# Weight sums of w1 and w2 made at their conversion, and another order of matmuls in the last group of u times w_out

## The chip, the cores and the metric

The kernel runs on one core of a Trainium2 chip. The core has a tensor engine for matmuls (PE, with PEld for its weight loads), a vector engine (DVE), a scalar engine (ACT), GpSimd (POOL) and SyncE (SP), from whose queue this kernel starts its DMAs. Each engine works through its own list of instructions in order and waits at semaphores for the others. Matmuls read their operands from the on-chip memory SBUF and write to PSUM. The metric is the device time of one execution in microseconds (us).

## The reference

```
p_packed = softmax_attention(p, k, v)          # 8 batches x 8 heads, 32 pack rows, width 64
attn     = softmax_attention(q, p_packed, p_packed)
x  = attn as [4608, 512]                        # 8 x 576 tokens
x  = (silu(x @ w_gate) * (x @ w_val)) @ w_out   # d_ff 1536
y  = ((x @ w1) * (x @ w2)) @ w3 @ w_out2        # d_ff 1024
```

q, k, v and p are float32. The weights of both expert layers arrive as 64-bit floats and are turned into float32 on the chip.

## The kernel before, in words

**Numbers.** Every large product is made with three matmuls: each factor is split into a high part (a cast on ACT, names ending in h) and a low part (the difference, on DVE or POOL, names ending in l), and high x high, high x low and low x high are added up in PSUM. The splits of most tiles are made by the helper `split` (L93) with `sub` (L89), so they carry those lines in the profile.

**First expert layer.** The 8 batches are worked off in 4 pairs P, and for each pair d_ff is cut into 12 tiles f of 128. A step is one (P, f). In it, `c_mm` (L409) makes c, a small product of the packed attention with w_gate and w_val, for the next tile; ACT casts it to ch (L420) and DVE subtracts to cl. For each of the two batches of the pair `stage1` makes the gate's product pg and the value's product pv (L441, 12 matmuls of 288 columns each), ACT takes Silu of pg (L446), DVE multiplies by pv (L450) and the result u is split into uh (ACT) and ul (POOL). Three tiles f make a group g of `stage3` (L660): u of these three times w_out, six PSUM tiles px (j = 0 to 5) of 18 matmuls of 384 columns. Each px is then added to acc (L682), and after the last group stored to a DRAM buffer X2d. `stage3` of a group runs in the step after the group's last tile, in two halves; so of three steps two are short (7.6 us) and one is long. The last group of the last pair has no step after it and runs in a loop of its own (L938).

All of pc, pg, pv, px and the small products pw of the next layer share one PSUM pool `ps` with four buffers of two banks.

**Conversions beside it.** Weights still to be converted go through a list `raw_q`: loaded by SP into a "raw" buffer (five of them), converted by `conv` with one operation on ACT (L346) and two on DVE (L347, L350). In the second and third pair one tile of w1 or w2 is converted per step (16 tiles of 128 x 512, `w12_conv`), from the second pair's tile 3 to the third pair's tile 6, and stored to a DRAM buffer w12d.

**Second expert layer.** Stage 5 works in 6 token groups g, and in each over 8 tiles f of 128 (for w1 and w2 together), by a scheme of seven products (`PROD`): instead of eight block products with w1 and w2, seven with the blocks A11, A12, A22 and the sums S1 to S4 of the blocks. A product is 6 matmuls of 384 columns (L981), so a tile f has 42. In group 0 the sums (`ws_sums`, L770 to L773, DVE) and the seven splits (`ws_block`: ACT casts, DVE and POOL subtract in turn) of tile f+1 are made while tile f runs, and are stored to wsd; from group 1 on they are loaded from there (`ws_load`). ACT takes results out of PSUM (s, L996), DVE and POOL combine them. The token side, x2r loaded from X2d, goes through `x2_prep` (sums on DVE, splits on ACT and DVE); that of group 0 is made in the last steps of the fourth pair. Stage 7 (L1035) multiplies by w3 @ w_out2 (L1045, 144 matmuls of 512 columns per group).

**The order.** Up to the end of the first layer a scheduler that is part of the framework sets each engine's order, from its own estimates and from a few pins in the program (`pin`). Stage 5 and 7 stand in `tc.manual_schedule`, where each engine's order is that of the code.

Of the kernel before, what the change touches and what calls it, by code (L numbers as in the profile page):

```python
# [38 lines left out]
def packed_attention_moe_kernel(  # L39
# [40 lines left out]
    GF = 3  # L80
# [20 lines left out]
    w12d = tc.dram_tile([NF2, 128, 2, ND, 128], F32, name="w12d")  # L101
# [180 lines left out]
    w12_list = [(x, c, h) for h in range(2) for x in range(2) for c in range(ND)]  # L282
# [12 lines left out]
    def raw_src(key):  # L295
        what, *at = key.split("_")
        at = [int(x) for x in at]
        if what == "wo2":
            c, kk = divmod(at[0], NH)
            return w_out2[512 * c:512 * c + 512, :].rearrange("(i k a) n -> k i a n", k=NH, a=32)[kk]  # L300
        if what == "w3":
            c, r = at
            return w3[128 * r:128 * r + 128, 512 * c:512 * c + 512].rearrange(
                "(b rr) (i n) -> i b rr n", rr=4, i=4)
        if what == "w":
            return (w_gate, w_val)[at[1]][:, 128 * at[0]:128 * at[0] + 128].rearrange(
                "(k p) n -> p k n", p=128)
        if what == "wo":
            return w_out[128 * at[0]:128 * at[0] + 128, :]
        x, c, h = w12_list[at[0]]  # L310
        return (w1, w2)[x][128 * c:128 * c + 128, 512 * h:512 * h + 512]
# [5 lines left out]
    def raw_load():  # L317
        if raw_at[0] < len(raw_q):
            key = raw_q[raw_at[0]]
            src = raw_src(key)  # L320
            raw_at[0] += 1
            blocks = src.shape[0] == 4
            t = vc.tile([128, 512] if blocks else [128] + list(src.shape[1:]), I64, tag="raw",
                        name=f"raw_{key}", bufs=5)
            if blocks:
# [5 lines left out]
            raw_t.append((key, t))  # L331

    def conv(key, t):
# [23 lines left out]
        if not in_front[0]:  # L357
            raw_load()
# [300 lines left out]

    def stage3(P, g, e):  # L660
        for j in range(ND // 2 * 3 // 2 * e, ND // 2 * 3 // 2 * (e + 1)):
            t = psum(f"px{P}_{g}_{j}")
            for n in range(GF):
                f = GF * g + n
                uh, ul = (x.rearrange("p b a s -> p (b a s)") for x in u_pair[P, f])
                wh, wl = wo_t[P, f]
                for w, x, first, last in (
                    (wh, uh, n == 0, False), (wh, ul, False, False), (wl, uh, False, n == GF - 1),
                ):
                    for h in range(2):  # L670
                        d, c = divmod(2 * j + h, 3)
                        nc.tensor.matmul(  # L672
                            t[:, h, 0:CW], lhsT=w[:, 128 * d:128 * d + 128], rhs=x[:, CW * c:CW * c + CW],
                            start=first, stop=last,
                        )
            if g == 0:
                o = up.tile([128, 2, CW], F32, tag=f"acc{j}", name=f"acc{P}_{j}", bufs=1)
                nc.scalar.copy(o, t[:, :, 0:CW])
                acc[j] = o
            else:  # L680
                o = acc[j]
                nc.vector.tensor_tensor(out=o, in0=o, in1=t[:, :, 0:CW], op=ALU.add)  # L682
            if g == NG - 1:
                for h in range(2):
                    d, c = divmod(2 * j + h, 3)
                    t0 = 2 * S * P + CW * c
                    if j % 3 == 1:
                        nc.sync.dma_start(X2d[d, :, t0:t0 + CW], o[:, h])
                    elif h == 0:
                        nc.sync.dma_start(X2d[d, :, t0:t0 + 2 * CW], o.rearrange("p h s -> p (h s)"))  # L690


    def w12_conv(i):
        x, c, h = w12_list[i]
# [62 lines left out]
    x2_t, x2r_t, w12r_t, wsrc, ws_t, wg_at = {}, {}, {}, {}, {}, []  # L757

    def load_w12(f):
        t = xp.tile([128, 2, 2, 256], F32, tag="wf", name=f"w12r{f}")  # L760
        nc.sync.dma_start(t.rearrange("p x k n -> p x (k n)"), w12d[f].rearrange("p x c n -> p x (c n)"))
        w12r_t[f] = t

    def ws_sums(f):
        t = w12r_t.pop(f)
        a11, a12, a21, a22 = (t[:, x, kh] for x in range(2) for kh in range(2))
        sa = vl.tile([128, 2, 256], F32, tag="vu", name=f"wsa{f}")
        sb = vl.tile([128, 2, 256], F32, tag="vu", name=f"wsb{f}")
        tt = nc.vector.tensor_tensor
        tt(out=sa[:, 0], in0=a21, in1=a22, op=ALU.add)  # L770
        tt(out=sa[:, 1], in0=sa[:, 0], in1=a11, op=ALU.subtract)
        tt(out=sb[:, 0], in0=a11, in1=a21, op=ALU.subtract)
        tt(out=sb[:, 1], in0=a12, in1=sa[:, 1], op=ALU.subtract)  # L773
        wsrc[f] = {"A11": a11, "A12": a12, "A22": a22, "S1": sa[:, 0], "S2": sa[:, 1],
                   "S3": sb[:, 0], "S4": sb[:, 1]}
# [11 lines left out]
    def ws_block(f, k):  # L787

        t = ws_tile(0, f, k)
        split(t[:, 0], t[:, 1], wsrc[f][PROD[k][1]], sub_on="pool" if k % 2 else "dve")  # L790
        if f:
            nc.sync.dma_start(wsd[f, k], t.bitcast(F32).rearrange("p h (d n) -> p h d n", d=2))

    def ws_load(g, f, k):
        t = ws_tile(g, f, k)
        nc.sync.dma_start(t.bitcast(F32).rearrange("p h (d n) -> p h d n", d=2), wsd[f, k])
# [60 lines left out]
    for n, (P, f) in enumerate(steps):  # L857
# [59 lines left out]
        if P == NPR - 1:  # L917
# [53 lines left out]
    def stage5(g, f):  # L971
# [79 lines left out]
    load_wo3(0)  # L1051
    with tc.manual_schedule(engines=M0):
        for g in range(NG2):
            for f in range(NF2):
                stage5(g, f)
                if g == 0:
                    if f + 2 < NF2:
                        ws_sums(f + 2)
                    if f + 3 < NF2:
                        load_w12(f + 3)  # L1060
# [47 lines left out]
```

## Time and profile before

| | before |
|---|---|
| time, median of 3 runs | 1379.38 us (1378.85 to 1380.13) |
| profiled execution: time | 1378.52 us |
| profiled execution: span | 1376.7 us |
| mean granted clock of PE | 0.995 |
| busy share: PE, DVE, ACT, POOL | 98%, 48%, 42%, 28% |
| DMA | 230.28 MB, mean 167 GB/s |

PE is busy nearly all the time; the others have half of their time free. The page's chain of work that ended last lies on PE for 85% of the span. Times in the rows below are from the span's start, in microseconds. Neighbouring instructions of one kind are drawn together in a timeline: its "x2" at the end counts them, and the second number is their time together. A bracket at the end of a row is the idle time before it and what ended it.

### The profile page before, as it was taken

To read this page: it belongs to the slowest core of one execution; us is meant where nothing else is said; L and a number is where in the kernel's file an instruction comes from. 1 tells how busy PE (TensorE), PEld (TensorE's weight loads), DVE (VectorE), ACT (ScalarE), POOL (GpSimd) and SP (SyncE) were. 2 spreads that over 40 slices of the span, in tenths; PEclk is the share of its full clock that TensorE was granted. 3 is DMA by queue.
4 is the path that set the end of the run, shared out by engine and by line. 5 is a ranking of instruction groups with operands and counts; after the bars stand their busy time and mean duration, and the time that the engine had idled before them with its cause. 6 is when DMAs were issued, how large, how long until landed. Compare 5 with 4: busy or idle time off the path is not lost.

```text
span 1376.7 us, 25585 instructions
## 1 busy us (share of the span) xinstructions
PE 1344.1 (98%) x10196; PEld 1235.3 (90%) x10196; DVE 658.7 (48%) x962; ACT 572.3 (42%) x956; POOL 386.0 (28%) x309
## 2 busy tenths in 40 slices
PE   6889999999999999999999999999999999999998
PEld 4669899999999999999898989989899899898997
DVE  2875867346563466462354378733413333234230
ACT  4784644235432444344544136433323233233231
POOL 0323322323322233253443226502112022021120
PEclk9999999999999999999999999999999999999999
DMA  9997766534455444145343238928548367285441
GB/s 281 314 268 212 228 188 200 153 97 133 125 127 181 124 135 123 55 144 148 120 130 104 82 121 308 347 70 254 173 131 254 105 198 231 74 253 170 132 152 46
DMA packets 195335, 230.28 MB, mean 167 GB/s; under 512 B 71056, under 2 KB 128400, under 8 KB 195216
## 3 DMA queue, kind: packets, MB, share of 16 engines
q1 hardware_dynamic: 195216, 228.64, 53.8%
q8 instruction: 81, 1.33, 0.4%
q14 instruction: 38, 0.31, 0.1%
HBM read 179.04 MB, written 49.55 MB: 166 GB/s over the span
## 4 chain that ended last, share of the span: by engine, by line
PE 85%; POOL 1%; DVE 1%; ACT 1%; issue 0%; DVEq 0%; POOLq 0%; ACTq 0%
PE px L672 20%; PE pA L981 15%; PE po L1045 14%; PE pg L441 10%; PE pv L441 9%; PE pB L981 7%; PE pC L981 4%; PE pc L409 3%; PE pw L736 3%; PE psq L206 1%; POOL wo2l L89 0%; POOL ul L89 0%; DVE u L450 0%; DVE xB21l L89 0%; ACT vt_wo L346 0%
## 5 line engine op out<-in xcount | busy, mean ns | idle before, releaser
L89 POOL TENSOR_TENSOR ul<-u,uh 128x576 fp32r<-128x576 f32 x96 | 146.7, 1528 | 329.3 <-ACT uh L93 324.2
L1001 POOL TENSOR_TENSOR c<-s,s 128x384 f32<-128x384 f32 x48 | 49.2, 1024 | 375.7 <-ACT s L996 375.5
L672 PE MATMUL px<-uh,woh 128*128 128x384 f32 x576 | 148.0, 337 | 2.4 <-DVE acc L682 1.4
L672 PE MATMUL px<-ul,woh 128*128 128x384 f32 x576 | 147.8, 337 | 2.5 <-POOL ul L89 2.5
L672 PE MATMUL px<-uh,wol 128*128 128x384 f32 x576 | 147.2, 336 | 0.0
L996 ACT COPY s<-pA 128x384 f32<-128x384 f32 x144 | 69.2, 481 | 182.6 <-PE pA L981 181.2
L450 DVE TENSOR_TENSOR u<-u,pv 128x576 f32<-128x576 f32 x96 | 71.8, 749 | 108.1 <-PE pv L441 98.2
L93 ACT CAST uh<-u 128x576 fp32r<-128x576 f32 x96 | 64.6, 673 | 115.1 <-DVE u L450 114.8
L682 DVE TENSOR_TENSOR acc<-acc,px 128x768 f32<-128x768 f32 x72 | 68.1, 948 | 92.4 <-PE px L672 92.2
L1045 PE MATMUL po<-wo_hi,abl 128*128 128x512 f32 x288 | 112.2, 390 | 0.0
L1045 PE MATMUL po<-wo_lo,abh 128*128 128x512 f32 x288 | 112.2, 389 | 0.0
L1045 PE MATMUL po<-wo_hi,abh 128*128 128x512 f32 x288 | 112.0, 389 | 0.0
L672 PEld LDWEIGHTS px<-uh,woh 128*128 128x128 f32 x576 | 103.5, 189 | 5.3 <-DVE acc L682 1.9
L672 PEld LDWEIGHTS px<-ul,woh 128*128 128x128 f32 x576 | 104.8, 189 | 3.1 <-POOL ul L89 3.1
L672 PEld LDWEIGHTS px<-uh,wol 128*128 128x128 f32 x576 | 104.9, 189 | 0.0
L89 DVE TENSOR_TENSOR abl<-ab,abh 128x768 fp32r<-128x768 f32 x48 | 48.6, 1013 | 105.1 <-ACT abh L93 105.1
L89 POOL TENSOR_TENSOR wol<-wof,woh 128x512 fp32r<-128x512 f32 x48 | 63.2, 1330 | 108.2 <-ACT woh L93 105.5
L441 PE MATMUL pg<-aTh,ch 128*128 128x288 f32 x384 | 87.2, 308 | 2.1 <-ACT u L446 1.2
L446 ACT ACTIVATE u<-pg 128x576 f32<-128x576 f32 x96 | 62.5, 651 | 60.6 <-PE pg L441 59.1
L441 PE MATMUL pv<-aTh,ch 128*128 128x288 f32 x384 | 82.9, 297 | 0.9 <-DVE cl L89 0.6
L441 PE MATMUL pg<-aTh,cl 128*128 128x288 f32 x384 | 82.3, 296 | 0.0
L441 PE MATMUL pv<-aTh,cl 128*128 128x288 f32 x384 | 82.2, 295 | 0.0
(309 smaller groups left out, 3099.0 us busy)
## 6 DMA issues: line engine op xcount, KB each, us to landing
ws<-wsd SPq DMA_DIRECT2D x245, 256.0 KB, 3.1
wf<-Wd SPq DMA_DIRECT2D x36, 512.0 KB, 4.8
wsd<-ws SPq DMA_DIRECT2D x49, 256.0 KB, 3.1
wof<-wod SPq DMA_DIRECT2D x36, 256.0 KB, 3.0
x2r<-X2d SPq DMA_DIRECT2D x24, 384.0 KB, 4.7
out_dram<-o SPq DMA_DIRECT2D x36, 256.0 KB, 2.0
km<-in_k_dram SPq DMA_DIRECT2D x16, 512.0 KB, 6.9
vm<-in_v_dram SPq DMA_DIRECT2D x16, 512.0 KB, 7.9
```

The lines of the kernel that those rows point to most:

```text
L89: return eng.tensor_tensor(out=out, in0=src, in1=hi.bitcast(F32), op=ALU.subtract)
L93: nc.scalar.copy(hi, src)
L409: nc.tensor.matmul(t[hs[at], b, Q], lhsT=PTd[es, 2 * (2 * P + b) + Q, hs[hq]], rhs=w[es, 2 * Q + hq // 2].rearrange("p g n -> p (g n)"), s ...
L441: nc.tensor.matmul(t[:, hf, 0:HS], lhsT=w[:, b % 2, Q, cols], rhs=x[:, Q, hf, :], start=first, stop=last,)
L446: x = nc.scalar.activation(u, t[:, :, 0:HS], AF.Silu)
L450: x = nc.vector.tensor_tensor(out=u, in0=u, in1=t[:, :, 0:HS], op=ALU.mult)
L672: nc.tensor.matmul(t[:, h, 0:CW], lhsT=w[:, 128 * d:128 * d + 128], rhs=x[:, CW * c:CW * c + CW], start=first, stop=last,)
L682: nc.vector.tensor_tensor(out=o, in0=o, in1=t[:, :, 0:CW], op=ALU.add)
L981: nc.tensor.matmul(bk[n], lhsT=w[:, hl, 128 * d:128 * d + 128], rhs=r[:, d], start=(first and d == 0 and i == 0), stop=(d == 1 and i == 2) ...
L996: nc.scalar.copy(o, t)
L1001: on.tensor_tensor(out=r, in0=o, in1=t, op=op)
L1045: nc.tensor.matmul(t, lhsT=a[:, j, cols], rhs=w[:, f], start=first, stop=last)
```

## The change

**Sums at the conversion.** A tile of `w12_list` is now (f, d): the four 128 x 128 blocks of w1 and w2 that tile f of stage 5 needs for its output half d, loaded by four DMAs of 128 KB. After its conversion `w12_blocks` makes S1 to S4 of it with four DVE operations of 128 columns, splits the three plain blocks (ACT, DVE) and the four sums (ACT, POOL), and stores them with seven DMAs of 128 KB to wsd. w12d, `load_w12`, `ws_sums` and `ws_block` are gone, and group 0 of stage 5 loads its weights from wsd as the others do: those of tile 0 at the end of the fourth pair, of tile 1 ahead of stage 5, and then a tile ahead. Raw buffers are shared with the split blocks, so only two raw tiles are loaded ahead while this lasts (`raw_fill`).

**The last group.** `stage3_last` takes four PSUM tiles at once, runs tiles f = 9 and 10 for all four, then f = 11 for each with its eviction, and then the last two PSUM tiles as before.

```diff
-    w12_list = [(x, c, h) for h in range(2) for x in range(2) for c in range(ND)]
+    w12_list = [(f, d) for f in range(NF2) for d in range(2)]
...
+            if parts:
+                for i in range(4):
+                    nc.sync.dma_start(t[:, 128 * i:128 * i + 128], src[i])
...
+    def raw_fill():
+        if w12_at[0] == len(w12_list):
+            depth = 5
+        else:
+            depth = 2 if raw_q[raw_at[0]].startswith(("w12", "wo2")) else 5
+        while raw_at[0] < len(raw_q) and len(raw_t) < depth:
+            raw_load()
...
+    def stage3_last(P, g):
+        ahead = {j: psum(f"px{P}_{g}_{j}") for j in range(4)}
+        for j in ahead:
+            stage3_mm(P, g, j, ahead[j], range(GF - 1))
+        for j in range(ND // 2 * 3):
+            t = ahead.get(j) or psum(f"px{P}_{g}_{j}")
+            stage3_mm(P, g, j, t, range(GF - 1 if j in ahead else 0, GF))
+            stage3_out(P, g, j, t)
...
-        nc.sync.dma_start(
-            w12d[4 * h:4 * h + 4, :, x, c, :].rearrange("f p n -> p f n"),
-            t.rearrange("p (f n) -> p f n", n=128))
...
+    def w12_blocks(i):
+        f, d = w12_list[i]
+        t = w12_t.pop(i).rearrange("p (k n) -> p k n", k=4)
+        a11, a12, a22, a21 = (t[:, k] for k in range(4))
+        x = vl.tile([128, 4, 128], F32, tag="vu", name=f"w12s{i}")
+        s1, s2, s3, s4 = (x[:, k] for k in range(4))
+        tt = nc.vector.tensor_tensor
+        tt(out=s1, in0=a21, in1=a22, op=ALU.add)
+        tt(out=s2, in0=s1, in1=a11, op=ALU.subtract)
+        tt(out=s3, in0=a11, in1=a21, op=ALU.subtract)
+        tt(out=s4, in0=a12, in1=s2, op=ALU.subtract)
+        for src, k0, k1, on in ((t[:, 0:3], 0, 3, "dve"), (x, 3, 7, "pool")):
+            o = vc.tile([128, 2, k1 - k0, 128], F32R, tag="raw", name=f"w12p{i}_{k0}", bufs=5)
+            split(o[:, 0], o[:, 1], src, sub_on=on)
+            for k in range(k0, k1):
+                nc.sync.dma_start(wsd[f, k, :, :, d, :], o[:, :, k - k0].bitcast(F32))
+        w12_at[0] += 1
+        raw_fill()
...
             w12_conv(i)
             pin.clear()
+            w12_blocks(i)
...
-                load_w12(0)
-                ws_sums(0)
                 for k in range(7):
-                    ws_block(0, k)
-    for e in range(2):
-        stage3(*pend, e)
-        if e == 0:
-            load_w12(1)
-            ws_sums(1)
-            load_w12(2)
+                    ws_load(0, 0, k)
+    stage3_last(*pend)
...
-            if g == 0 and f + 1 < NF2:
-                ws_block(f + 1, k)
...
-            if f and 0 < ng < NG2:
+            if (f or g == 0) and ng < NG2:
                 ws_load(ng, nf + 1, k)
```

Three places where the engines' order changes are shown as the built programs have them; the numbers at the end of a name count tiles and buffers.

PE, the last group of the first layer, before: px_3_0 and px_3_1 are its first two PSUM tiles; uh_9 to uh_11 belong to tiles 9 to 11.

```order
L672 MATMUL px_3_0_9322<-uh_10_9153,woh_10_9099 128x384 x2
L672 MATMUL px_3_0_9322<-ul_10_9154,woh_10_9099 128x384 x2
L672 MATMUL px_3_0_9322<-uh_10_9153,wol_10_9100 128x384 x2
L672 MATMUL px_3_0_9322<-uh_11_9247,woh_11_9214 128x384 x2
L672 MATMUL px_3_0_9322<-ul_11_9248,woh_11_9214 128x384 x2
L672 MATMUL px_3_0_9322<-uh_11_9247,wol_11_9215 128x384 x2
L672 MATMUL px_3_1_9343<-uh_9_8831,woh_9_8748 128x384 x2
```

The same place now, from the end of the fourth PSUM tile's part with tiles 9 and 10.

```order
L684 MATMUL px_3_3_9629<-uh_10_9472,woh_10_9418 128x384 x2
L684 MATMUL px_3_3_9629<-ul_10_9473,woh_10_9418 128x384 x2
L684 MATMUL px_3_3_9629<-uh_10_9472,wol_10_9419 128x384 x2
L684 MATMUL px_3_0_9626<-uh_11_9566,woh_11_9533 128x384 x2
L684 MATMUL px_3_0_9626<-ul_11_9567,woh_11_9533 128x384 x2
L684 MATMUL px_3_0_9626<-uh_11_9566,wol_11_9534 128x384 x2
```

The first matmul with tile 11 stood behind 12 of px_3_0 and stands behind 48 of px_3_0 to px_3_3 now.

DVE, second pair, from tile 4's last u to tile 5's, before: vx and w12t are the conversion of a tile of w1 or w2, cl_6 belongs to the next tile's c.

```order
L450 TENSOR_TENSOR u_4_4164<-u_4_4164,pv_4_4179 128x576
L347 TENSOR_SCALAR vx_w_1_4196<-raw_w_1_3135 128x512
L350 SCALAR_TENSOR_TENSOR w12t_4195<-w12t_4195,vx_w_1_4196 128x512
L89 TENSOR_TENSOR cl_6_4226<-pc_6_4208,ch_6_4225 128x1024
L450 TENSOR_TENSOR u_5_4229<-u_5_4229,pv_5_4244 128x576
```

Now, with the sums w12s (four) and the split w12p of the three plain blocks:

```order
L464 TENSOR_TENSOR u_4_4185<-u_4_4185,pv_4_4200 128x576
L361 TENSOR_SCALAR vx_w_1_4217<-raw_w_1_3398 128x512
L364 SCALAR_TENSOR_TENSOR w12t_4216<-w12t_4216,vx_w_1_4217 128x512
L736 TENSOR_TENSOR w12s_4226<-w12t_4216 128x128
L738 TENSOR_TENSOR w12s_4226<-w12t_4216 128x128
L737 TENSOR_TENSOR w12s_4226<-w12s_4226,w12t_4216 128x128
L89 TENSOR_TENSOR w12p_0_4231<-w12t_4216,w12p_0_4231 128x384
L739 TENSOR_TENSOR w12s_4226<-w12t_4216,w12s_4226 128x128
L89 TENSOR_TENSOR cl_6_4267<-pc_6_4249,ch_6_4266 128x1024
L464 TENSOR_TENSOR u_5_4270<-u_5_4270,pv_5_4285 128x576
```

Five operations stand between the conversion and cl.

On ACT, at the same place, the cast of the three plain blocks (w12p_0, from w12t) now stands ahead of ch_6, and the cast of the four sums between ch_6 and the Silu of u_5; before, ch_6 followed the last cast of u_4.

SP at the end of the fourth pair, before: part and w3o belong to the product of w3 and w_out2, x2r are the token blocks of group 0.

```order
L731 DMA part_9071<-wo3d 128x512
L743 DMA wo3d<-w3o_6_9061 128x512
L743 DMA wo3d<-w3o_7_9085 128x512
L801 DMA x2r_00_9093<-X2d 128x2x384
L801 DMA x2r_01_9095<-X2d 128x2x384
```

Now:

```order
L778 DMA part_9390<-wo3d 128x512
L790 DMA wo3d<-w3o_6_9380 128x512
L790 DMA wo3d<-w3o_7_9404 128x512
L819 DMA ws_6_9624<-wsd 128x512
L824 DMA x2r_00_9412<-X2d 128x2x384
L824 DMA x2r_01_9414<-X2d 128x2x384
```

The last of tile 0's seven ws loads stands ahead of the x2r loads.

## Rows read from the trace of the kernel before

**Rows 1.** Waits of PE, 800 to 1377 us: waited for, total us, times, longest

```profile
PE px L672 <- POOL ul L89: 2.5, 2, 1.5
PE px L672 <- ACT uh L93: 1.0, 2, 0.7
```

**Rows 2.** Timeline of PE, 800 to 814 us: start, us, instruction, idle before

```profile
801.62 0.51 PE L672 MATMUL px<-uh,wol 128*128 128x384 f32 x2
...
807.03 0.69 PE L672 MATMUL px<-ul,woh 128*128 128x384 f32 x1 [1.47 <-POOL ul L89]
...
811.96 0.51 PE L672 MATMUL px<-uh,woh 128*128 128x384 f32 x2
```

**Rows 3.** Two stretches: length, busy us of PE to POOL, PE clock, DMA

```profile
802.00:808.00 6.00, 2.59 (x7) 1.55 (x7) 6.00 (x6) 2.17 (x3) 4.09 (x2) 0.76 0.00 0
808.00:812.00 4.00, 4.00 (x15) 4.00 (x14) 1.52 (x2) 0.71 (x2) 0.18 (x1) 0.51 0.72 231
```

**Rows 4.** Timeline of POOL, 795 to 812 us

```profile
802.89 4.09 POOL L89 TENSOR_TENSOR ul<-u,uh 128x576 fp32r<-128x576 f32 x2 [4.00 <-ACT uh L93]
```

**Rows 5.** Timeline of DVE, 795 to 812 us

```profile
801.37 1.40 DVE L450 TENSOR_TENSOR u<-u,pv 128x576 f32<-128x576 f32 x2
...
805.64 2.15 DVE L89 TENSOR_TENSOR xT4l<-x2T,xT4h 128x768 fp32r<-128x768 f32 x1
```

**Rows 6.** Chain that ended last, 830 to 1050 us: start, us, what

```profile
832.02 2.12 PE pA L981 x12
...
885.50 32.78 PE po L1045 x144
...
924.52 2.08 PE pA L981 x12
...
976.52 32.68 PE po L1045 x144
```

**Rows 7.** Groups by line, whole span: count, busy, mean ns, idle before

```profile
L981 PEld LDWEIGHTS pA<-xT3h,ws 128*128 128x128 f32 x192 | 35.4, 188 | 1.6 <-ACT s L996 1.6
```

**Rows 8.** Views of one line or tile: ns shortest/median/longest, first and last start

```profile
L772 DVE TENSOR_TENSOR wsb<-w12r x8: 410/418/421, 814.4 to 873.2; 128x256 f32<-128x256 f32 x8
...
L89 DVE TENSOR_TENSOR xT3l<-x2T,xT3h x6: 944/958/960, 807.7 to 1265.2; 128x768 fp32r<-128x768 f32 x6
...
L93 ACT CAST wo_hi<-wo3r x8: 615/620/622, 832.3 to 888.1; 128x512 fp32r<-128x512 f32 x8
...
L697 SPq DMA_DIRECT2D w12d<-w12t x16: 370/382/389, 306.6 to 520.0; - x16
```

**Rows 9.** Costliest groups, part 5 of the page

```profile
L89 POOL TENSOR_TENSOR ul<-u,uh 128x576 fp32r<-128x576 f32 x96 | 146.7, 1528 | 329.3 <-ACT uh L93 324.2
...
L89 POOL TENSOR_TENSOR wol<-wof,woh 128x512 fp32r<-128x512 f32 x48 | 63.2, 1330 | 108.2 <-ACT woh L93 105.5
```

**Rows 10.** Timeline of DVE: tile 5 and 11 of pair 2, 5 of pair 3

```profile
326.55 1.21 DVE L89 TENSOR_TENSOR cl<-pc,ch 128x1024 fp32r<-128x1024 f32 x1
...
410.14 1.23 DVE L89 TENSOR_TENSOR cl<-pc,ch 128x1024 fp32r<-128x1024 f32 x1 [0.53 <-ACT ch L420]
...
496.98 1.23 DVE L89 TENSOR_TENSOR cl<-pc,ch 128x1024 fp32r<-128x1024 f32 x1 [0.40 <-ACT ch L420]
```

**Rows 11.** Timeline of PE in the same steps

```profile
328.50 0.42 PE L441 MATMUL pv<-aTh,ch 128*128 128x288 f32 x2
...
413.47 0.42 PE L441 MATMUL pv<-aTh,ch 128*128 128x288 f32 x2
...
499.05 0.42 PE L441 MATMUL pv<-aTh,ch 128*128 128x288 f32 x2
```

**Rows 12.** DMA issues, part 6 of the page: count, KB, us to landing

```profile
ws<-wsd SPq DMA_DIRECT2D x245, 256.0 KB, 3.1
```

**Rows 13.** A quiet short step: length, busy us of each engine, PE clock

```profile
407.73:415.33 7.60, 7.60 (x88) 6.89 (x81) 3.77 (x5) 4.12 (x6) 3.35 (x3) 1.00 0.61 179
```

**Rows 14.** Waits of PE, 100 to 800 us

```profile
PE px L672 <- DVE acc L682: 1.4, 1, 1.4
```

More of the change, by code (lines that the diff above doesn't have):

```diff
@@ L100, in packed_attention_moe_kernel @@
     wod = tc.dram_tile([NF, 128, DM], F32, name="wod")
-    w12d = tc.dram_tile([NF2, 128, 2, ND, 128], F32, name="w12d")
     wsd = tc.dram_tile([NF2, 7, 128, 2, 2, 128], F32, name="wsd")
@@ L309, in raw_src @@
             return w_out[128 * at[0]:128 * at[0] + 128, :]
-        x, c, h = w12_list[at[0]]
-        return (w1, w2)[x][128 * c:128 * c + 128, 512 * h:512 * h + 512]
+        f, d = w12_list[at[0]]
+        return [(w1, w2)[x][128 * (2 * kh + d):128 * (2 * kh + d) + 128, 128 * f:128 * f + 128]
+                for x, kh in ((0, 0), (0, 1), (1, 1), (1, 0))]
     raw_at = [0]
@@ L321, in raw_load @@
             raw_at[0] += 1
-            blocks = src.shape[0] == 4
-            t = vc.tile([128, 512] if blocks else [128] + list(src.shape[1:]), I64, tag="raw",
+            parts = isinstance(src, list)
+            blocks = not parts and src.shape[0] == 4
+            t = vc.tile([128, 512] if blocks or parts else [128] + list(src.shape[1:]), I64, tag="raw",
                         name=f"raw_{key}", bufs=5)
-            if blocks:
+            if parts:
+                for i in range(4):
+                    nc.sync.dma_start(t[:, 128 * i:128 * i + 128], src[i])
+            elif blocks:
                 for i in range(4):
@@ L331, in raw_load @@
             raw_t.append((key, t))
+    def raw_fill():
[5 more added lines that the diff above has]
+            raw_load()
+    w12_at = [0]
     def conv(key, t):
@@ L357, in conv @@
         if not in_front[0]:
-            raw_load()
+            raw_fill()
     wf_t, wst_t = {}, {}
@@ L658, in packed_attention_moe_kernel, with stage3_mm, stage3_out @@
     CW = 2 * S // 3
+    def stage3_mm(P, g, j, t, ns):
+        for n in ns:
+            f = GF * g + n
+            uh, ul = (x.rearrange("p b a s -> p (b a s)") for x in u_pair[P, f])
+            wh, wl = wo_t[P, f]
+            for w, x, first, last in (
+                (wh, uh, n == 0, False), (wh, ul, False, False), (wl, uh, False, n == GF - 1),
+            ):
+                for h in range(2):
+                    d, c = divmod(2 * j + h, 3)
+                    nc.tensor.matmul(
+                        t[:, h, 0:CW], lhsT=w[:, 128 * d:128 * d + 128], rhs=x[:, CW * c:CW * c + CW],
+                        start=first, stop=last,
+                    )
+    def stage3_out(P, g, j, t):
+        if g == 0:
+            o = up.tile([128, 2, CW], F32, tag=f"acc{j}", name=f"acc{P}_{j}", bufs=1)
+            nc.scalar.copy(o, t[:, :, 0:CW])
+            acc[j] = o
+        else:
+            o = acc[j]
+            nc.vector.tensor_tensor(out=o, in0=o, in1=t[:, :, 0:CW], op=ALU.add)
+        if g == NG - 1:
+            for h in range(2):
+                d, c = divmod(2 * j + h, 3)
+                t0 = 2 * S * P + CW * c
+                if j % 3 == 1:
+                    nc.sync.dma_start(X2d[d, :, t0:t0 + CW], o[:, h])
+                elif h == 0:
+                    nc.sync.dma_start(X2d[d, :, t0:t0 + 2 * CW], o.rearrange("p h s -> p (h s)"))
     def stage3(P, g, e):
@@ L662, in stage3 @@
             t = psum(f"px{P}_{g}_{j}")
[L663 to L690, printed above, removed]
+            stage3_mm(P, g, j, t, range(GF))
@@ L693, in w12_conv @@
+            stage3_out(P, g, j, t)
[6 more added lines that the diff above has]
+            stage3_mm(P, g, j, t, range(GF - 1 if j in ahead else 0, GF))
+            stage3_out(P, g, j, t)
     def w12_conv(i):
-        x, c, h = w12_list[i]
+        f, d = w12_list[i]
         t = vl.tile([128, 512], F32, tag="vu", name=f"w12t{i}")
@@ L696, in w12_conv @@
         conv(f"w12_{i}", t)
-        nc.sync.dma_start(
-            w12d[4 * h:4 * h + 4, :, x, c, :].rearrange("f p n -> p f n"),
-            t.rearrange("p (f n) -> p f n", n=128))
+        w12_t[i] = t
+    w12_t = {}
+    def w12_blocks(i):
+        f, d = w12_list[i]
+        t = w12_t.pop(i).rearrange("p (k n) -> p k n", k=4)
[13 more added lines that the diff above has]
+        w12_at[0] += 1
+        raw_fill()
@@ L756, in packed_attention_moe_kernel @@
             ("A", "S3", "T3"), ("C", "A12", "B21"), ("A", "A22", "T4"))
[L757 to L775, printed above, removed]
+    WSK = [("A11", "A12", "A22", "S1", "S2", "S3", "S4").index(name) for _, name, _ in PROD]
+    x2_t, x2r_t, ws_t, wg_at = {}, {}, {}, []
     def ws_tile(g, f, k):
@@ L785, in ws_tile @@
         return t
[L787 to L792, printed above, removed]
     def ws_load(g, f, k):
         t = ws_tile(g, f, k)
-        nc.sync.dma_start(t.bitcast(F32).rearrange("p h (d n) -> p h d n", d=2), wsd[f, k])
+        nc.sync.dma_start(t.bitcast(F32).rearrange("p h (d n) -> p h d n", d=2), wsd[f, WSK[k]])
     def x2_load(g, i, j):
@@ L1051, in packed_attention_moe_kernel @@
     load_wo3(0)
+    for k in range(7):
+        ws_load(0, 1, k)
     with tc.manual_schedule(engines=M0):
@@ L1056, in packed_attention_moe_kernel @@
                 if g == 0:
[L1057 to L1060, printed above, removed]
                     split_wo3(f)
```

## The prediction

> **What bounds the kernel now.** I read the page first: the tensor engine (PE) is busy for 98% of the span, so a change can only win where PE idles or runs slowly, or lose by making PE wait. I therefore went to the waits of PE, then to the timeline around the longest ones, then to the granted clock of that stretch, and last to the neighbours on the other engines whose work the change moves.
>
> After 800 us PE waits in one place only, at the matmuls of u with w_out, for ul from GpSimd (POOL) and for uh from the scalar engine (ACT) [rows 1]. It is the last group of u times w_out, after all steps. There the matmul pair of tile 10 starts at 801.62 and would be over at 801.97 at the usual pitch; tile 11 then needs uh and ul of the step that has just ended. The reader is to see that PE reaches the first full-rate pair again at 811.96 [rows 2]. Between lie 18 matmuls (four single ones, then seven pairs, the first of them at 807.51), and in the second half of it the clock is at 0.51, the lower of its two levels, 1.2 GHz instead of 2.4; before it PE had been idle for more than half of 6 us, and the mean clock of those 6 us was already 0.76 [rows 3]. The usual pitch comes from the stage after it: 12 matmuls of 384 columns in 2.08 us, 0.1733 us each [rows 6].
>
> Why the data are late: the last u comes out of the vector engine (DVE) at 801.37 + 1.40 = 802.77 [rows 5], because the x2 preparation stands before it on DVE; its two ul run on POOL from 802.89 to 806.98 [rows 4].
>
> **Part 1, the last group in another order.** Before, PE needs uh of tile 11 right at 801.97. Now four PSUM tiles take tiles 9 and 10 first: 48 matmuls where 12 stood, 36 more, 36 x 0.1733 = 6.24 us. uh of tile 11 is needed at 808.21 and ul two matmuls later, at 808.55; it is there at 806.98, so 1.57 us are left. The matmuls' number is the same. What this removes is 811.96 - 801.97 = 9.99 us for 18 matmuls, less the 18 x 0.1733 = 3.12 us they need at full rate: 6.87 us.
>
> What is late next: four PSUM tiles held at once need all four buffers. The third, px_3_2, takes the buffer of the last step's first pv, which u of that batch gives free; that is the first of the two u, about 802.1, and PE comes there 12 matmuls after 801.97, at 804.05. The fourth takes the second pv's buffer, free at 802.77 and wanted at 806.1. No wait there. Evictions of px_3_0 to px_3_3 now come closer together, one each 6 matmuls (1.04 us), and an addition to acc takes the 0.95 us of a 768-column operation [rows 8]; the fifth tile waits for the first eviction only, three tiles back.
>
> The cover can be lost through SP's queue. Of the seven ws loads for stage 5, the last now stands on SP ahead of the four loads of x2r, and the x2 preparation that waits for x2r stands ahead of u on DVE. It waits for PE to be done with the last wf tile, and costs one issue, 0.38 us [rows 8], up to one whole 256 KB load, 3.1 us [rows 12]. I take 1 us, nearer to the issue since loads overlap: u, uh and ul come 1 us later, 0.57 us of the 1.57 remain. At 3.1 us PE would wait 1.5 us again.
>
> **Part 2, stage 5's first token group.** In group 0, ACT, DVE and POOL make sums and splits of the next tile's weights beside the seven products; from group 1 on they are only loaded. From the same place (the last product of the first tile) to the start of the next stage, group 0 takes 885.50 - 832.02 = 53.48 us, group 1 takes 976.52 - 924.52 = 52.00 us [rows 6]: 1.48 us. What ends PE's wait there is ACT's eviction s, 1.6 us in all [rows 7], and ACT now has the 49 casts less. So -1.48 us. The loads that replace them are seven of 256 KB in each tile's 7.28 us, which is what groups 1 to 5 do already in their 52 us. For the second tile all seven stand on SP behind the end of the last group; they are wanted 7.28 us after stage 5 starts, and the first go out as soon as the old u space is free, some 3 us before. The bound: if one comes a full 3.1 us late [rows 12], the term is +1.6 instead of -1.48.
>
> **Part 3, the work that comes in the second and third pair.** Per tile of w1, w2 (16 of them): on DVE four operations of 128 columns and one of 384. By the line through 256 columns (0.418) and 768 columns (0.958) [rows 8] that is 0.28 each and 0.55: 4 x 0.28 + 0.55 = 1.67, with the same rounding up 1.7 us. On ACT two casts of no more than 512 columns, at most 0.62 each, 1.24 us; on POOL one of 512 columns, 1.33 us [rows 9]; on SP eleven issues instead of two, 9 x 0.38 = 3.4 us. None of the engines is full: a short step lasts 7.6 us. So only the order counts.
>
> The new work has one deadline. On DVE it stands ahead of cl, the split of the next tile's c (the DVE rows shown with the change), and cl is the last reader of a PSUM buffer that the step's second pv needs. Three places show the margin. In a quiet step cl runs from 410.14 to 411.37 and the pv starts at 413.47: 2.1 us [rows 10, 11]. cl waited there 0.53 us for ch, so DVE had been free since 409.61, and 1.7 us more make it start at 411.3 and end at 412.5: still 0.9 us in time. In the second pair's tile 5 there is no such idle time: cl runs from 326.55 to 327.76, the pv starts at 328.50; with 1.7 it ends at 329.46, 0.96 late. In the third pair's tile 5 cl starts at 496.98 after 0.40 of idle time, ends at 498.21, and the pv starts at 499.05: 498.21 + 1.7 - 0.40 = 499.51, 0.46 late. Two steps late, 0.96 + 0.46 = 1.4 us. This is the value I take.
>
> The change also adds a wait on ACT. The cast of the first three blocks waits for the converted tile from DVE, and ch of the next tile is queued behind it, then the second cast, then Silu. In the second pair's tile 5 the converted tile is there at 326.55; a cast of 0.62 and ch, which like cl has 1024 columns (I take cl's 1.2), end at 328.4, 0.1 after DVE gets to cl anyway. A second cast and a Silu of about that length end near 329.6. The buffer that Silu frees is wanted by the next step's pc, behind the 12 matmuls of the second pv (288 columns, 12 x 0.13 = 1.6 us after 328.50), at 330.1 or later. So the wait costs next to nothing beyond the 0.96.
>
> On POOL the new subtraction stands among the ul, whose readers come a group later. On SP the seven stores wait for DVE and POOL, with loads of wf and wof behind them; wf has four buffers, so a load has three steps, over 20 us, before its tile is wanted. I cost both at nothing; if that cover is gone, a late wf is one landing late, 3 to 5 us, once.
>
> What the trace before does not show is how long the added operations take with POOL at work. Bounds from the rows: two ul that ran beside the x2 preparation took 4.09 us, 2.05 each against a mean of 1.53 [rows 4, 9], and the subtraction xT4l took 2.15 against 0.958 [rows 5, 8]. So the 1.7 us on DVE can become 3.4, or, with POOL idle, stay. Below nothing the term can go by the waits that are there now and may be shifted away, the longest of them that lies in a group's additions being 1.4 us [rows 14]. The ends of this term are -1.4 and +10.8 (worked out in the first rival).
>
> The Trainium skill, "GPSIMD Engine Reference", section "1. Specifications", states that GpSimd shares its SBUF interfaces with VectorE and that they contend when a DVE instruction has two SBUF inputs. All five added DVE operations are of that kind, and the change puts a sixth subtraction on POOL right behind them, so the rule speaks against part 3; the trace agrees, by the 4.09 and 2.15 us above. By the rule alone every added operation would be stretched and the sum would come out near 1382, as in the first rival's upper end; POOL is busy for 3.35 of the 7.60 us of a quiet step [rows 13], so the rows bear it out for a part of them.
>
> **The sum.** The profiled execution took 1378.52 us. 1378.52 - 6.87 - 1.48 + 1.4 = 1371.57. The median of the runs, 1379.38, lies 0.86 above it, so I predict 1372.4 us.
>
> **Rivals.**
> 1. Contention between DVE and POOL eats the gain. At double length DVE is 1.7 us later still: the two tight steps lose 0.96 + 1.7 and 0.46 + 1.7, 4.8 us; a quiet step is 1.7 - 0.9 = 0.8 late. Of the ten short steps with a tile eight are quiet. With half of them hit, 4.8 + 4 x 0.75 = 7.8 us: 1378.52 - 8.35 + 7.8 + 0.86 = 1378.8, no change. With all, 10.8 us: 1381.8. For it speaks the 2.15; against it, that POOL is idle for 4.2 of a quiet step's 7.6 us [rows 13].
> 2. Slower, by a circle between DVE and ACT in the short steps. The cast waits for DVE's conversion, the second cast for DVE's sums, Silu stands behind it on ACT, and DVE's next u waits for Silu. In a quiet step DVE is busy for 3.77 us and ACT for 4.12 [rows 13]; with the added 1.7 and 1.24 that is 10.8 us, and if the two only ever waited for each other, the step would take that instead of 7.6. It decides once the ten short steps with a tile are longer by 1.1 us each, since that costs the 8.35 gained and 2.8 more. Half way to the full circle, 1.6 us in each: 1378.52 - 8.35 + 16 + 0.86 = 1387.0. For it speaks that in the tight steps the two do follow each other without a gap; against it, that no more than two short steps stand in a row, and the long step behind them, with 6 x 18 matmuls of u times w_out, 18.7 us of them, more for PE, lets both engines catch up.
> 3. The cover in the last group is lost, by the ws load ahead of x2r: 1.5 us of waiting, and about as much again at the lower clock, as before (3.4 us of waiting, 6.87 lost): 1372.4 + 3.0 = 1375.4.
>
> **How the numbers follow.** A measurement of this kernel can tell some 0.2%, 2.8 us, from no change. My forecast gets 0.56, with a range of its own of 1370 to 1374.5 (the unknown 1.4 to each side, and 1 us more for part of the contention). The first rival gets 0.19, the second 0.11, the third 0.14. Faster than 1376.6: forecast and third rival, 0.70; within: most of the first, 0.18; slower: the second and the end of the first, 0.12. The range goes from 1369.5 (forecast less the 1.4 that waits now there may give, and the rest of the spread of the runs) to 1380.5, which leaves out the second rival and the upper end of the first.
>
> **What would show it.** Part 1: in the changed kernel's waits no ul or uh in the last group, the clock at 1.00 through it, and one pitch from the first px to stage 5. Part 2: the same 52.0 us in group 0 as in group 1, no wait for s. Part 3: in the second and third pair new waits of pv for cl, near 1 and 0.5 us in the two steps named; the added DVE operations at 0.28 and 0.55. I am wrong if PE waits for cl or u in most short steps, if DVE's added operations are at twice their length, or if x2T starts over 2.5 us later and the last group idles again.

## The result: slower by 1%, and the profile after

| | before | after |
|---|---|---|
| time, median | 1379.76 us (4 runs, 1378.85 to 1380.22) | 1392.46 us (4 runs, 1392.35 to 1395.67) |
| ratio | | 1.0099 (95% interval 1.0081 to 1.0116) |
| profiled execution: time, span | 1378.52, 1376.7 us | 1392.58, 1390.8 us |
| busy share: PE, DVE, ACT, POOL | 98%, 48%, 42%, 28% | 97%, 47%, 41%, 27% |

Forecast were 1372.4 us and a range of 1369.5 to 1380.5. The first gain came as it was worked out, the second at three quarters of it; the work moved into the second and third pair cost fourteen times what I gave it.

To see where the time goes, I took from each timeline the start of pc, one per step, and subtracted the same start in the kernel before. The difference stays constant where nothing changes, so each stretch has its own price. All columns are profiled executions; "head" is the attention of the first 107 us, whose loads differ by up to 3 us between these executions, also between kernels with the same order there (before, e1, e5, e8: 2.3 us); e1 to e8 are the experiments below.

```
us against before         after    e1     e2     e3     e4     e5     e6     e7     e8
head                       1.70  -1.13   0.21  -0.58   0.33   1.21   1.81  -0.35  -1.07
rest of pair 1             1.46   0.01   1.41   1.42   1.46   0.04   1.45   1.47  -0.01
pairs 2, 3 with tiles     19.58  -0.01  20.37   7.96  14.14  23.76   4.34   3.62   0.00
  pair 2, tile 5           2.65   0.00   4.03   3.24   0.33   4.05   0.00   0.29   0.00
  pair 2, tile 7           2.42   0.00   2.20   0.00   1.20   2.23   0.01   0.00   0.01
  pair 2, tiles 10, 11     4.49   0.01   4.01   0.07   6.16   4.97   0.00   0.00   0.00
  pair 3, tile 2           6.37   0.00   5.92   0.82   3.40   7.05   0.47   0.00   0.00
  pair 3, tiles 4, 5       3.41  -0.01   3.69   2.65   1.53   3.32   0.54   1.60   0.00
rest of 3, and pair 4     -0.84  -0.45  -1.21  -1.20  -1.21  -0.10  -1.13  -1.15   0.16
```

After these rows come the last group, from the last pc to stage 5: 785.96 to 825.66 before, 807.86 to 840.67 after, 39.70 against 32.81 us, so -6.89; and stage 5's group 0 from there to its first po, 59.84 before and 58.73 after, -1.11. 1.70 + 1.46 + 19.58 - 0.84 - 6.89 - 1.11 = 13.9 of the 14.06 us between the two profiled executions.

**The last group.** The chain that ended last in the changed kernel answers to [rows 2 and 6] (start, length, what):

```profile
821.94 18.73 PE px L684 x108
...
840.67 1.06 PE pA L998 x6
841.73 1.30 PE pB L998 x6
...
847.19 2.08 PE pA L998 x12
...
899.40 32.68 PE po L1060 x144
```

The reader is to see one piece of 108 matmuls without a break: 18.73 / 108 = 0.1734 us each, the full rate. ul comes as late as before [rows 4], from 824.80 to 828.94 (timeline of POOL in the changed kernel); it is wanted at 821.94 + 50 x 0.1734 = 830.6, with 1.7 us to spare against the 1.57 worked out.

```profile
824.80 4.14 POOL L89 TENSOR_TENSOR ul<-u,uh 128x576 fp32r<-128x576 f32 x2 [4.00 <-ACT uh L93]
```

The clock of the stretch stays at 1.00 where it was 0.76 [rows 3] (length, busy us of PE to POOL, PE clock, DMA):

```profile
824.00:830.00 6.00, 6.00 (x37) 6.00 (x36) 6.00 (x6) 2.18 (x3) 4.14 (x2) 1.00 0.00 0
```

From 847.19 to 899.40 group 0 takes 52.21 us, against 53.48 [rows 6], and group 1 now takes the same, from 938.33 to 990.54:

```profile
938.33 2.08 PE pA L998 x12
...
990.54 32.68 PE po L1060 x144
```

**What was lost.** The waits of PE from 240 to 560 us, a stretch in which PE waited for nothing before (who waits, for whom: total us, times, longest):

```profile
PE pv L455 <- ACT u L460: 14.1, 6, 3.0
PE pv L455 <- DVE cl L89: 0.6, 1, 0.6
```

Six times a pv waits for Silu, and once, for 0.6 us in the third pair's tile 4, for cl. Two chains lead there, each to three of the six. The first, in the second pair's tile 5, in the timelines of DVE, ACT and PE of the changed kernel:

```profile
329.91 1.75 DVE L364 SCALAR_TENSOR_TENSOR w12t<-w12t,vx_w 128x512 int32<-128x512 int32 x1
...
332.37 0.55 DVE L89 TENSOR_TENSOR w12p<-w12t,w12p 128x384 fp32r<-128x384 f32 x1
332.84 0.28 DVE L739 TENSOR_TENSOR w12s<-w12t,w12s 128x128 f32<-128x128 f32 x1
```

```profile
331.69 0.51 ACT L93 CAST w12p<-w12t 128x384 fp32r<-128x384 f32 x1 [2.08 <-DVE w12t L364]
332.11 1.00 ACT L434 CAST ch<-pc 128x1024 fp32r<-128x1024 f32 x1
333.20 0.62 ACT L93 CAST w12p<-w12s 128x512 fp32r<-128x512 f32 x1
333.73 0.64 ACT L460 ACTIVATE u<-pg 128x576 f32<-128x576 f32 x1
```

```profile
334.42 0.53 PE L455 MATMUL pv<-aTh,ch 128*128 128x288 f32 x2 [2.41 <-ACT u L460]
```

ACT stands 2.08 us before the cast, for DVE's conversion; ch, the second cast and Silu follow, and the pv starts 0.05 us after Silu's end. pg had long been there. (cl ends at the same moment, 333.14 + 1.22; but the semaphore that this pv waits for is one that ACT raises, not DVE.) The third pair's tile 5 goes the same way.

The second chain begins on SP. Its waits in the second and third pair (first row), and the timelines of SP, ACT and PE in the second pair's tile 10:

```profile
SPq L744 <- DVE w12s L739: 77.2, 15, 14.7
```

```profile
405.19 4.77 SPq L744 DMA_DIRECT2D wsd<-w12p  x7
410.00 2.04 SPq L328 DMA_DIRECT2D raw_w<-in_moe_w_dram  x4
412.15 1.11 SPq L403 DMA_DIRECT2D wof<-wod  x2
```

```profile
415.99 0.62 ACT L93 CAST woh<-wof 128x512 fp32r<-128x512 f32 x1 [5.35 <-DMA wof<-wod]
416.51 0.64 ACT L460 ACTIVATE u<-pg 128x576 f32<-128x576 f32 x1
```

```profile
417.21 0.53 PE L455 MATMUL pv<-aTh,ch 128*128 128x288 f32 x2 [2.72 <-ACT u L460]
```

The stores at 405.19 had waited for DVE's last sum; seven stores and four loads later, at 412.15, SP issues the load of wof, 3.8 us before ACT can cast it, and Silu is queued behind that cast. The wait alone is nothing new: in the kernel before, SP waited for DVE in the same stretch, too, ahead of raw loads and of the stores of w12, and PE lost nothing by it:

```profile
SPq L330 <- DVE vx_w L347: 45.4, 7, 15.2
SPq L697 <- DVE w12t L350: 26.6, 11, 11.5
```

What is new is the wait with 7.0 us of issuing between it and a load that is wanted soon. By these rows (an estimate) a load of wof issued at 405.19 and landing 3.8 us later would have been there by 409.0, and PE stood only from 414.49 on.

In the second pair's tile 7 it is this chain again. In the third pair's tile 2 PE waits twice, 1.4 us behind wof and then 3.0 us by the first chain: DVE's u, and the conversion behind it, had waited for the first, late Silu. After such waits the clock falls, too: PE was idle for 2.5 us of 466 to 472, and from 472 to 478 us the granted clock was 0.72, so the five places of the table cost more than the 14.1 us waited.

### The profile page after: what moved, and what is told of

Same layout as the page of the kernel before. It is cut to its first block, busy times and chain, and to the rows that moved or that the text cites. A ratio compares the mean times of both kernels' runs of the same rounds, so it can differ in the third digit from the quotient of the medians.

```text
span 1390.8 us, 25800 instructions
## 1 busy us (share of the span) xinstructions
PE 1347.9 (97%) x10196; PEld 1236.5 (89%) x10196; DVE 659.6 (47%) x978; ACT 570.0 (41%) x932; POOL 380.5 (27%) x301
## 4 chain that ended last, share of the span: by engine, by line
PE 79%; DVE 5%; ACT 2%; issue 2%; POOL 2%; DMA 1%; SPq 1%; DVEq 0%; ACTq 0%; POOLq 0%
PE px L684 18%; PE pA L998 14%; PE po L1060 14%; PE pv L455 8%; PE pg L455 8%; PE pB L998 7%; PE pC L998 4%; PE pw L783 3%; PE pc L423 2%; DMA wof<-wod 1%; DVE w12t L364 1%; PE psq L205 1%; DVE u L464 1%; ACT u L460 1%; POOL wo2l L89 0%
## 5 line engine op out<-in xcount | busy, mean ns | idle before, releaser
L455 PE MATMUL pv<-aTh,ch 128*128 128x288 f32 x384 | 84.4, 302 | 15.1 <-ACT u L460 14.1
L455 PE MATMUL pv<-aTl,ch 128*128 128x288 f32 x384 | 82.9, 298 | 0.0
```

The source lines that it names most:

```text
L455: nc.tensor.matmul(t[:, hf, 0:HS], lhsT=w[:, b % 2, Q, cols], rhs=x[:, Q, hf, :], start=first, stop=last,)
```

## The experiments

The theory after the result: two waits of one engine for another, each with something else queued behind it, make up the 19.6 us: ACT's casts for DVE (ahead of Silu), and SP's stores for DVE (ahead of wof). Rivals: the added work and its contention on DVE and POOL, or the traffic of the small DMAs; and that the parts work on each other.

**e1, the last group alone.** The kernel before with `stage3_last`:

```diff
+            if j == 2:
+                load_w12(1)
+                ws_sums(1)
+                load_w12(2)
...
-    for e in range(2):
-        stage3(*pend, e)
-        if e == 0:
-            load_w12(1)
-            ws_sums(1)
-            load_w12(2)
+    stage3_last(*pend)
```

> The kernel before with the new order of the last group alone (the loads and sums of w12 that stood between the halves of the last group now stand behind its third PSUM tile). Theory: the last group's gain is independent of the rest and the first three pairs run as in before, 1379.6 - 6.9 = 1372.7 us, last pc to stage 5 in 32.8 us instead of 39.7, no wait of PE in it. Rival: the gain needed the engines that the sums left free; with the sums of tile 0 still on DVE, ACT and POOL behind the last u, acc of the first PSUM tile comes late and part is given back: 1375 to 1377 us with PE waiting for acc.

Measured: 1379.49 us, ratio 0.9992 (0.9981 to 1.0004): no gain at all beyond the noise. Everything up to the last group runs as in before (table), and the last group takes 38.35 us, 1.35 less. The rival held, more strongly than put. The waits of PE, over the whole span, and the timelines of DVE and PE in that stretch:

```profile
PE px L670 <- DVE acc L682: 5.3, 2, 3.9
```

```profile
809.52 0.43 DVE L788 TENSOR_TENSOR wsa<-w12r 128x256 f32<-128x256 f32 x1 [2.38 <-DMA w12r<-w12d]
...
812.95 0.94 DVE L89 TENSOR_TENSOR ws<-w12r,ws 128x256 fp32r<-128x256 f32 x1
813.82 1.80 DVE L682 TENSOR_TENSOR acc<-acc,px 128x768 f32<-128x768 f32 x2
```

```profile
814.81 1.01 PE L670 MATMUL px<-uh,woh 128*128 128x384 f32 x2 [3.86 <-DVE acc L682]
```

DVE waits for the load of w12 and makes the sums of tile 0 first; acc of the first PSUM tile comes behind them, and with all four PSUM tiles held the fifth has none. So the gain of the new order needs DVE free for acc: in the changed kernel the sums are gone from there, and e8 tries the other way.

**e2, the sums alone.** The changed kernel with the old last group.

```diff
-    stage3_last(*pend)
+    for e in range(2):
+        stage3(*pend, e)
```

> The changed kernel with the last group in its old order. Theory (the parts are independent): 1392.5 + 6.9 = 1399.4 us, the same late steps in the second and third pair (about 19.6 us over before) and the same 3 us in the first pair. Rival (the last group's order shifted the scheduler's placing of the rest): the steps of pairs 1 to 3 differ from the changed kernel's, time anywhere from 1380 to 1399 us.

Measured: 1399.33 us, ratio 1.0137 (1.0112 to 1.0161). The theory's number: the moved work costs the same without the new last group, 20.4 us in pairs 2 and 3. The last group in its old order is 0.81 us shorter here than before, with the sums gone.

**e3, stores that wait for nothing.**

```diff
-        nc.sync.dma_start(t, wod[f])
+        wof_at.append(nc.sync.dma_start(t, wod[f]))
...
-                nc.sync.dma_start(wsd[f, k, :, :, d, :], o[:, :, k - k0].bitcast(F32))
+                x = nc.sync.dma_start(wsd[f, k, :, :, d, :], PTd[:, 0:2])
+                tc.add_manual_dep(x.ins, wof_at[-1].ins.name, NO_SYNC, reason="behind the wof load")
```

> The changed kernel, its seven stores per tile of w1, w2 taken from a tile that is long there (the packed attention), so stage 5 works with other weights; number, size and runs of the DMAs stay, only SP's wait for DVE and POOL goes. Theory (SP's wait ahead of the wof loads makes wof, woh on ACT and the Silu behind it late in three steps): those steps lose nothing, about 10 us less, 1382.5 us; the steps where ACT waits for the converted tile stay late (about 9 us over before). Rival (the small DMAs themselves, by their traffic, make wof late): no change, 1391 to 1394 us.

Measured: 1380.36 us, ratio 1.0001 (0.9991 to 1.0012). Of the 19.6 us, 7.96 are left. Tiles 7, 10 and 11 of the second pair lose nothing more, and tile 2 of the third 0.82 instead of 6.37, with the same number, size and runs of stores; the two tiles 5 stay late by 3.24 and 2.58. Its waits of PE from 240 to 560 us:

```profile
PE pv L455 <- ACT u L460: 5.3, 3, 2.4
```

So stores that no longer stand waiting ahead of wof are worth 11.6 us here, the first chain's wait in the third pair's tile 2 included, and the stores' traffic is not the cause. The edit takes away two things at once: the wait, and the stores' place, since they now go behind the last load of wof (a load at 405.41, seven stores from 405.78). Which of the two would have been enough is not shown.

**e4, the casts on DVE.**

```diff
-            split(o[:, 0], o[:, 1], src, sub_on=on)
+            split(o[:, 0], o[:, 1], src, on="dve", sub_on=on)
```

> The changed kernel with the high parts of the new blocks made on DVE instead of ACT. Theory (ACT's casts wait for DVE and hold up ch and Silu): the three steps with 2.4 to 3.0 us of waiting for Silu behind such a cast lose nothing, about 9 us less, 1383.5 us, though DVE has two more operations per tile. Rival (DVE itself is the limit, its operations stretched beside POOL): DVE gets longer still, those steps stay late or get later, 1392 to 1397 us, with PE waiting for cl or u.

Measured: 1387.80 us, ratio 1.0053 (1.0032 to 1.0074): the direction of the theory, 5.4 us in pairs 2 and 3 instead of 9. The two tiles 5 lose 0.33 and 1.07 instead of 2.65 and 2.67, although DVE has more to do. But tile 4 of the second pair is now 1.68 late, with PE waiting for cl, and the wof places, which this edit leaves, still cost 10.8 us for 13.3 (tile 2 of the third pair, where both chains meet, 3.0 less; tiles 10 and 11 of the second 1.7 more).

**e5, raw tiles one at a time in the first pair.**

```diff
+        if w12_at[0] == 0 and not (raw_q[raw_at[0]].startswith("w12")):
+            return raw_load()
```

> The changed kernel, but each conversion of the first pair loads one raw tile again, as before the change, instead of filling up to five. Theory (the scheduler ordered the first pair otherwise because the raw tiles came earlier; one long step there lost 3.05 us, of which 1.6 came back): the first pair runs as in before, 1.4 us less, 1391 us, and the late steps of pairs 2 and 3 stay. Rival (that step was late by the attention's loads, whatever the order): its 3 us stay, 1392.5 us.

Measured: 1394.24 us, ratio 1.0104 (1.0072 to 1.0137). For the first pair the theory held: one step there cost 3.06 us in every kernel with the new `raw_fill`, and costs nothing here; 0.04 are left of 1.46. The time is a miss all the same: the later order moved, too, and pairs 2 and 3 lost 23.8.

**e6, one step later.** Sums, splits and stores of a tile in the next step, with DVE's sums pinned behind cl and ACT's casts behind that step's first Silu.

```diff
+            behind(nc.vector.tensor_tensor(**kw), "dve")
...
+            behind(nc.scalar.copy(o[:, 0], src), "act")
...
+            act_at = pin_at.get("act")
             stage1(2 * P, f, 1)
+        if 0 <= n - NF - 4 < len(w12_list):
+            pin.clear()
+            pin.update(act=act_at, dve=pin_at["cl"])
+            w12_blocks(n - NF - 4)
...
-            w12_blocks(i)
```

> The changed kernel with sums, splits and stores of a tile made one step later, DVE's sums behind cl and ACT's casts behind the first Silu of that step. Theory: ACT no longer waits for DVE ahead of ch and Silu, so the waits for Silu behind a cast go (5.4 us by the run with the casts on DVE), while SP still waits for DVE ahead of wof loads: 1385 to 1388 us. Rival (there is too much work for DVE and ACT in a short step, wherever it stands): as many late steps as in the changed kernel, 1391 us or more.

Measured: 1376.71 us, ratio 0.9973 (0.9958 to 0.9988), faster than before, with all the added work, DMAs and stores in place. Better than the theory put it, and SP's wait ahead of the stores is shorter as well: 16.8 us for DVE and 14.7 for POOL in place of 77.2 and 4.7; why it is was not tried. The rival (too much work, wherever it stands) falls: pairs 2 and 3 lose 4.3 us. DVE's added operations also got shorter here, 2 of the 64 over 1 us where in the changed kernel it was the first of twelve tiles (the last section), so this run alone does not part the waits from the contention. PE's waits of that stretch:

```profile
PE px L684 <- DVE sT L212: 1.7, 2, 0.8
PE pg L455 <- ACT u L460: 1.1, 2, 0.7
PE pv L455 <- DVE cl L89: 0.4, 1, 0.4
```

**e7, both waits away.** The edits of e3 and e4 together.

> Both edits at once: stores from a tile that is long there (so stage 5 works with other weights) and the high parts of the blocks on DVE. Theory (two separate waits, ACT's for DVE and SP's for DVE, make up the loss): 1392.5 - 11.6 - 5.4 = 1375.5 us, pairs 2 and 3 at most 3 us longer than in before. Rival (DVE and POOL contending is what makes the steps late): 1380 us or more, steps late with PE waiting for cl or u.

Measured: 1374.93 us, ratio 0.9969 (0.9955 to 0.9983). The theory's 1375.5: 3.6 us left in pairs 2 and 3. PE's waits there are for cl, what the prediction had feared, 2.3 us of them for its 1.4, though in the two tiles 4 (1.43 and 1.34 us late) and with more work on DVE:

```profile
PE pv L455 <- DVE cl L89: 2.3, 2, 1.2
PE pc L423 <- DVE cl L89: 0.4, 2, 0.2
```

The contention is still there, with 13 of the 16 first operations over 1 us, so it is not what cost the 19.6 us (count, ns shortest/median/longest):

```profile
L736 DVE TENSOR_TENSOR w12s<-w12t x16: 292/1226/1339, 308.0 to 524.8; 128x128 f32<-128x128 f32 x16
```

In e3, e4 and e7 the last group keeps 5.68 of its 6.89 us, as stage 5's first product waits 1.0 us for the last addition to acc.

**e8, the last group with acc first.** The kernel before with `stage3_last`, and the sums of stage 5's tile 0 pinned on DVE behind acc of the fourth PSUM tile.

```diff
+            if j == 3:
+                pin.clear()
+                pin["acc"] = pin_at["acc"]
+                ws_sums(0)
+                for k in range(7):
+                    ws_block(0, k)
+                load_w12(1)
+                load_w12(2)
+        pin["acc"] = pin_at["acc"]
+        ws_sums(1)
+        pin.clear()
...
```

The pin puts DVE's sums and splits behind that addition.

> The kernel before with the new order of the last group, and the sums and splits of stage 5's tile 0 pinned on DVE behind acc of the fourth PSUM tile, those of tile 1 behind the last acc. Theory (the order of the last group gains its 6.9 us once DVE serves acc first; in the run with the last group alone PE waited 5.3 us for acc behind those sums): 1379.9 - 6.9 = 1373.0 us. Rival (the sums are late then and stage 5 waits for them instead): 1376 us or more, with PE waiting for ws at the start of stage 5.

Measured: 1372.64 us, ratio 0.9944 (0.9926 to 0.9961), faster than both kernels, and 7.1 us under the median of before, 6.89 of them in the last group. Its chain:

```profile
799.12 18.73 PE px L670 x108
```

From the last pc, at 785.04, to the end of that piece at 817.85 are 32.81 us, as in the changed kernel, and its waits of PE show none for acc or ws there.

## Why the prediction was wrong

- **The last group (-6.87): right.** -6.89, with the margin of ul as worked out; the third and fourth PSUM tile waited for nothing. Not seen was that this rested on DVE being free for acc: with the sums of tile 0 still ahead of it the order alone gave 1.35 (e1), with them behind it 6.89 (e8).
- **Stage 5's group 0 (-1.48): right within 0.4.** Group 0 takes as long as group 1 now, 52.21 us, as was said, 1.27 less than before; from the start of stage 5 it is -1.11, with a longer piece at its second product, 1.30 us for 1.06.
- **The third part (+1.4): this failed, with +19.6 and 1.5 more in the first pair.** Three sentences of it.
- *"On SP the seven stores wait for DVE and POOL ... I cost both at nothing."* I gave wf's four buffers as the cover, and passed over wof, whose load is issued one step ahead, with two buffers, and whose cast stands ahead of Silu on ACT. e3 prices this at 11.6 us. The "late wf, one landing, 3 to 5 us, once" was of about the right size per place, but it came three times, by wof: 2.4, 4.5 and 6.4 us. SP's issues, priced at 0.38 us each, took 0.68 and 0.51: 6.8 us per tile.
- *"The buffer that Silu frees is wanted by the next step's pc."* It is wanted by the same step's second pv: the wait is for Silu, and cl, the deadline I worked with, added one wait of 0.6 us, in another step. In the tiles 5 the second pv takes the first pg's buffer, in both kernels: its semaphore is ACT's. It is in the tiles 4 that it takes pc's and waits for cl (the 0.6 us, and e7). With that, my own 329.6 for Silu against 328.50 for the pv would have said 1.1 us in this step, not nothing. The step was the one named (tile 5 of both pairs), and measured 2.65 and 2.67. e4 and e7 show that this wait goes when the casts leave ACT.
- *Of the size*, DVE's conversion in the second pair's tile 5 began 1.7 us later than worked out: vx at 328.8 against 323.78 + 3.36 = 327.14. The chain that ended last goes back from there to the tile in the step before, whose sums stood ahead of that step's softmax on DVE (start, length, what):

```profile
310.15 1.05 DVE w12s L736
...
312.00 0.28 DVE w12s L739
312.28 1.26 DVE qmx L228
```

This is read from the chain, and wasn't tried by itself. In the third pair's tile 5 the conversion itself was longer, for the reason in the last section (DVE before, then after):

```profile
495.25 0.54 DVE L347 TENSOR_SCALAR vx_w<-raw_w 128x512 int32<-128x512 int32 x1
495.89 0.69 DVE L350 SCALAR_TENSOR_TENSOR w12t<-w12t,vx_w 128x512 int32<-128x512 int32 x1
```

```profile
515.56 1.53 DVE L361 TENSOR_SCALAR vx_w<-raw_w 128x512 int32<-128x512 int32 x1
517.20 1.72 DVE L364 SCALAR_TENSOR_TENSOR w12t<-w12t,vx_w 128x512 int32<-128x512 int32 x1
```

The five added operations took the 1.7 us forecast in both these tiles; in twelve of the sixteen they took 2.5 to 2.7.

- **The scheduler, not thought of.** `raw_fill` gave another order to the first pair, far from the tiles that it was changed for: 1.5 us (e5).
- **The rivals.** The second, a circle between DVE and ACT, had two of the three engines (not SP, which carries 11.6 of the 19.6 us) and the right sign, but as a step grown longer, not as a wait behind a wait; the first, contention, is a part of the size, not the cause (e7). The third did not come: ul kept its margin. (In the first one's sum, 4 x 0.75 should be 4 x 0.8, 0.2 us more.)

## What to carry to other kernels

Cheap work on idle engines is not free if it waits: price each added instruction by what is queued behind it on its engine when its data are late, one engine after the other, and SP's queue is one of them, with the time that SP needs to issue what stands between. Read from the built program which buffer a waiting tile really takes, rather than from the order in which the code asks for them. And try the parts one by one: here one part hid in the other's loss, and could be had alone only after a second look at what DVE did first.

## What the runs showed of the hardware

**A conversion or sum on DVE that starts while POOL runs a ul ends just after it.** The added 128-column operations took the 0.28 us forecast, but the first of a tile a median of 1.13 (form, count, ns shortest/median/longest):

```profile
L736 DVE TENSOR_TENSOR w12s<-w12t x16: 292/1131/1350, 310.1 to 542.8; 128x128 f32<-128x128 f32 x16
L738 DVE TENSOR_TENSOR w12s<-w12t x16: 276/279/286, 311.1 to 544.0; 128x128 f32<-128x128 f32 x16
```

In all twelve tiles where it took over 1 us, it began within a ul on POOL and ended 0.14 to 0.16 us after the ul's end; in the other four the conversion before it did so instead (1.72 to 1.92 us for 0.69, ending some 0.55 us after the ul). One of them, DVE above and POOL below:

```profile
384.94 1.12 DVE L736 TENSOR_TENSOR w12s<-w12t 128x128 f32<-128x128 f32 x1
```

```profile
384.00 1.92 POOL L89 TENSOR_TENSOR ul<-u,uh 128x576 fp32r<-128x576 f32 x1 [0.63 <-ACT uh L93]
```

So the added operations are not stretched one by one: the first is held, and the next run at full speed once POOL is done. A tile's five operations took 1.13 + 3 x 0.28 + 0.55 = 2.5 us at the median, not 1.7 (each begins some 0.08 us before the one ahead ends, so from first start to last end it is 2.2 us, and 1.37 where none is held). The Trainium skill, "SBUF — State Buffer", section "Who interferes with whom", states that a DVE instruction with two SBUF inputs contends with a GpSimd instruction that reads SBUF, over a shared port pair that works as an exclusive lock; its section "Summary: rules for kernel authors" adds that the second one to issue is fully blocked until the first has finished. The rows agree, for DVE as the second. The prediction had taken the contention for a stretching of every operation.

**SP's issue costs go neither by the bytes nor by the number of runs.** Seven stores of 128 KB in runs of 512 bytes took SP 4.77 us, 0.68 each, and four loads of 128 KB in runs of 1 KB 2.04, 0.51 each: 6.8 us of SP per tile, in a step of 7.6. But the store of w12d before took 0.38 [rows 8] with twice the bytes and, by the DMA records of the trace, twice the runs, 512 of 512 bytes. What sets the cost is not shown; a row for the same form of transfer is needed to price one.
